# Matmuls on zeros before the first tile, w2 loaded behind the first seven x tiles, and the h3T tile placed first in its pool, in a one-core attention and MLP kernel

## The chip, the cores and the metric

The kernel runs on one core of a Trainium2 chip. The metric is the device time of one execution in microseconds (us). One execution moves by a few us from run to run (six runs of the unchanged kernel: 1540.59 to 1544.17 us). Each kernel also has one profiled execution. Its trace gives the start and length of every instruction, what ended each wait, and each DMA packet. Engines are named as in the profile: PE is TensorE (matmuls), PEld its weight loads, DVE VectorE, ACT ScalarE, POOL GpSimd, and SP the engine that issues most DMAs (SPq is its queue).

## The reference, cut to what matters

The result is the sum of x, a memory-augmented attention A and a block B, both fed by the layer norm of x. The change touches only B, which runs first:

```python
def _B_ref(x, w1, w2, w3, w4):                 # x is the layer norm of the input, 2048 x 1024
    h = _gelu(_layernorm(x) @ w1)              # stage 1
    # four quarters of h shifted by +1, -1, +2, -2 tokens
    hs = shifted(h) @ w2                       # stage 2
    x1 = x + hs
    return x1 + _gelu(_layernorm(x1) @ w3) @ w4   # stage 3 (w3, w4)
```

## The kernel before: the parts that matter

The 2048 tokens are 16 tiles of 128. In stage 1 every tile is normalized twice over (`xn2` for w1, `xn` kept for later), `xn2` is transposed, and PE multiplies by w1. Tiles 0 to 7 are transposed by PE, tiles 8 to 15 by DMA transposes issued from SP. Groups of tiles go through PE in order: tile 0, tile 1, then pairs (2,3), (4,5), and so on. PE must have tiles 8 and 9 transposed to start the sixth group. The trace calls the kept tile `xnk`; PE first reads it in a small matmul with `c_segsum` (sums over segments of tokens). `hTB` is what stage 1 writes, and the tiles `ps`, in PSUM, are what the matmuls write.

```python
load_x(0)
for c in range(2):
    nc.sync.dma_start(w1_sb[:, :, c * 512:(c + 1) * 512], w1_v[:, :, c * 512:(c + 1) * 512])
    load_x(c + 1)
for n in range(3, 7):
    load_x(n)
...
def norm1(n):                                   # xn of tile n; frees the buffer of x tile n
    ...
    nc.vector.tensor_scalar(xn, xts[n][:], mv[:, 0:1], rr[:, 0:1], op0=ALU.subtract, op1=ALU.mult)
    nc.gpsimd.dma_start(xn_v[:, n, :], xn)
    load_x(n + 7)
    if n < 4:
        nc.sync.dma_start(w2_sb[:, 2 * n:2 * n + 2, :], w2_v[:, 2 * n:2 * n + 2, :])
    elif n in (12, 15):
        load_w3()
...
norm_stats(0)                                   # DVE: statistics of x tile 0
xn2 = norm2(0, t0, 0)
norm_stats(1, 0)                                # DVE: first half of the statistics of tile 1
transposes(xn2, t0, 0, 0)                       # PE
transposes(xn2, t0, 0, 1, on_dve=True)          # PE, copied out by DVE
norm_stats(1, 1)
...
# stage 2, per tile: matmuls on w2, norm, then
    nc.scalar.activation(xn3[:], x1[:], ACTF.Identity, bias=nm3[:], scale=r3[:])
    nc.sync.dma_start_transpose(xn3T[n // 4][:, n % 4], xn3[:])
# stage 3 takes over the memory of stages 1 and 2
big = p3.enter_context(tc.tile_pool(name="p3big", bufs=1))
w4_sb = big.tile([P, FT, D], BF16)
...
h3T = big.tile([P, FT, 512], BF16)
...
    nc.scalar.activation(h3T[:, f, :], ps[:], ACTF.Gelu_apprx_tanh)   # after eight matmuls on w3
```

A tile pool is a stack region of on-chip memory. When a new pool lies where a closed one lay, the framework makes the first users of its tiles wait for the last users of the old memory.

## Time and profile before

| what | value |
|---|---|
| time, six runs | 1540.59 to 1544.17 us, median 1542.38 |
| span of the profiled execution | 1545.1 us |
| PE busy | 1514.8 us (98%) |
| first matmul on w1, w3, w4 | 8.23, 131.97, 181.93 us |

The first line of the page's part 1 reads: busy us, share of the span, instructions.

```profile
PE 1514.8 (98%) x10308; PEld 839.7 (54%) x10382; DVE 523.8 (34%) x1092; ACT 513.9 (33%) x1218; POOL 192.5 (12%) x272
```

PE is the limit, so only time in which PE waits, or runs slowly, can be won. The waits view of PE over the whole span (who waited for what: us in total, times, longest; some lines left out):

```profile
PE ps L283 <- DVE xn L262: 6.9, 1, 6.9
PE psO L678 <- DMA PT<-Pn: 3.8, 5, 1.6
PE ps L569 <- ACT Vs L571: 3.1, 1, 3.1
PE ps L300 <- DMA xn2T<-xn: 1.5, 1, 1.5
PE ps L515 <- ACT h3T L516: 1.1, 1, 1.1
PE ps L292 <- DVE xnk L271: 0.8, 1, 0.8
```

The three edits aim at three things seen here: the 6.9 us before PE's first instruction and the slow clock that follows it, the DMA traffic of the start, and the 1.1 us wait for h3T. The timeline shows each (start us, us, engine, line, operation, in brackets the idle time before it and its releaser). The start:

```profile
8.03 0.69 DVE L247 BATCH_NORM_STATS2 st<-xt 128x6 f32<-128x512 bf16 x1 [1.14 <-DMA xt<-in_A_x_dram]
9.37 3.15 PE L300 MATMUL ps<-xn2T,w_sb 128*128 128x128 bf16 x28 [0.55 <-DVE xn2T L285]
17.96 0.54 DVE L271 TENSOR_SCALAR xnk<-xt,mv,rr 128x1024 bf16<-128x1024 bf16 x1
18.55 0.35 PE L292 MATMUL ps<-c_segsum_sb,xnk 128*128 128x4 bf16 x8 [0.81 <-DVE xnk L271]
```

28 matmuls took 3.15 us, 112 ns each. Sixteen of the same shape at 18.77 us started 56 ns apart. The Trainium skill (TensorE: Matmul & The Clock Gate, "Part 1: The HAM clock gate") says that the array starts at half rate until it has been busy for a window of about 3.4 us. The trace's clock record agrees: full rate from 13.99 us on, after a window (10.58 to 13.99 us) in which PE was busy throughout. Yet at 18.55 us PE stands and waits for VectorE, whose chain began when x tile 1 landed at 8.03 us.

The one wait for a DMA transpose, and the h3T wait:

```profile
46.77 1.47 PE L300 MATMUL ps<-xn2T,w_sb 128*128 128x256 bf16 x12 [1.50 <-DMA xn2T<-xn]
139.45 2.06 ACT L516 ACTIVATE h3T<-ps 128x512 bf16<-128x512 f32 x4 [3.01 <-DMA xn3T<-xn]
140.10 1.24 PE L515 MATMUL ps<-xn3T,w_sb 128*128 128x512 bf16 x5 [1.06 <-ACT h3T L516]
```

The first line is PE's start on tiles 8 and 9. The other two say that ACT may not write h3T before the last xn3 transpose has landed, and that PE runs out of PSUM buffers meanwhile.

The windows view gives the DMA load. Columns: stretch, its length, busy us (and count) of PE, PEld, DVE, ACT, POOL, granted clock, mean busy share of the 16 DMA engines, GB/s.

```profile
12.00:14.00 2.00, 2.00 (x21) 2.00 (x20) 1.90 (x6) 1.30 (x3) 0.08 (x1) 1.00 0.54 205
14.00:16.00 2.00, 2.00 (x39) 2.00 (x37) 1.90 (x6) 1.17 (x6) 0.82 (x2) 1.00 0.00 0
28.00:30.00 2.00, 2.00 (x23) 1.82 (x21) 1.90 (x6) 1.24 (x3) 0.66 (x1) 1.00 1.07 383
```

DMA is idle around 15 us and full at 28 us, where the w2 loads run. (The clock column reads 1.00 before the first record of a change and says nothing there.)

### The profile page before, as it was taken

How to read it: one execution, taken by the hardware profiler on the slowest of the kernel's cores; microseconds unless marked ns; L12 is line 12 of the kernel's file. 1: busy time of each engine (PE TensorE's matmuls, PEld its weight loads, DVE VectorE, ACT ScalarE, POOL GpSimd, SP SyncE). 2: the span in 40 equal slices, each digit the busy share in tenths (PEclk: the TensorE clock that was granted, in tenths of full speed). 3: DMA queues.
4: the chain of work that ended last, by engine and by line, in shares of the span. 5: the costliest groups of instructions: out<-in, count | busy, mean ns of one | idle time of the engine just before them, and what ended most of it. 6: DMA issues, size and time to landing. Idle time of an engine off the chain costs nothing. (4 is left out here: it accounts for less than half of the span.)

```text
span 1545.1 us, 25390 instructions
## 1 busy us (share of the span) xinstructions
PE 1514.8 (98%) x10308; PEld 839.7 (54%) x10382; DVE 523.8 (34%) x1092; ACT 513.9 (33%) x1218; POOL 192.5 (12%) x272
## 2 busy tenths in 40 slices
PE   7999999999999999999999999999999999999998
PEld 7844444444444444444456645654665566466654
DVE  8284010000200111111246624651663365235541
ACT  5533202103012011111156614651662366056620
POOL 5232020221211241010000011002000200100001
PEclk9999999999999999999999999999999999999999
DMA  7679543452353998542389947992997599458611
GB/s 251 182 213 311 205 148 125 143 184 83 130 164 87 215 275 273 173 124 83 123 231 252 235 129 179 246 237 73 239 239 175 129 249 227 111 130 198 136 45 50
DMA packets 288601, 270.39 MB, mean 175 GB/s; under 512 B 137459, under 2 KB 255368, under 8 KB 288480
## 3 DMA queue, kind: packets, MB, share of 16 engines
q1 hardware_dynamic: 265088, 185.53, 47.0%
q0 software_dynamic: 23392, 83.19, 16.8%
q8 instruction: 83, 1.36, 0.4%
q14 instruction: 38, 0.31, 0.1%
HBM read 190.73 MB, written 46.73 MB: 154 GB/s over the span
## 5 line engine op out<-in xcount | busy, mean ns | idle before, releaser
L639 PE MATMUL ps<-hTb,wt 128*128 128x396 bf16 (+2 forms) x3072 | 514.9, 314 | 1.3 <-DMA wt<-in_A_Wq_dram 1.3
L639 PEld LDWEIGHTS <-wt 128*128 128x128 bf16 x3072 | 264.5, 97 | 148.1 <-DMA wt<-in_A_Wq_dram 2.1
L569 PE MATMUL ps<-wt,xT 128*128 128x512 bf16 x1004 | 222.0, 381 | 4.1 <-ACT Vs L571 3.1
L697 PE MATMUL pso<-wo_sb,oX 128*128 128x512 bf16 x1000 | 223.2, 379 | 1.4 <-issue 0.2
L515 PE MATMUL ps<-xn3T,w_sb 128*128 128x512 bf16 x896 | 195.9, 379 | 1.1 <-ACT h3T L516 1.1
L540 PE MATMUL ps<-w_sb,h3T 128*128 128x512 bf16 x872 | 194.3, 379 | 1.2
L569 PEld LDWEIGHTS <-xT 128*128 128x128 bf16 x1024 | 100.6, 98 | 125.3 <-issue 5.6
L516 ACT ACTIVATE h3T<-ps 128x512 bf16<-128x512 f32 x112 | 66.5, 597 | 292.0 <-PE ps L515 289.0
L697 PEld LDWEIGHTS <-oX 128*128 128x128 bf16 x1024 | 98.9, 98 | 115.3
L645 ACT CAST KT<-ps 128x396 bf16<-128x396 f32 (+1 forms) x192 | 87.1, 456 | 189.6 <-PE ps L639 186.5
L515 PEld LDWEIGHTS <-w_sb 128*128 128x128 bf16 x896 | 86.8, 98 | 103.9 <-issue 1.3
L540 PEld LDWEIGHTS <-h3T 128*128 128x128 bf16 x896 | 86.8, 98 | 102.8
L660 DVE TENSOR_REDUCE sums<-sm 99x4 f32<-99x396 f32 (+1 forms) x176 | 97.6, 555 | 113.9 <-ACT sm L658 113.9
L647 ACT ACTIVATE QT<-ps 128x396 bf16<-128x396 f32 (+1 forms) x192 | 89.4, 469 | 108.0 <-PE ps L639 79.8
L656 DVE TENSOR_TENSOR sm<-psS,c_mask_reg_sb 99x396 f32<-99x396 f32 x160 | 91.4, 572 | 90.1 <-PE psS L654 89.9
L571 ACT CAST Vs<-ps 128x512 bf16<-128x512 f32 x64 | 37.2, 586 | 238.4 <-PE ps L569 152.6
L658 ACT ACTIVATE sm<-sm 99x396 f32<-99x396 f32 (+1 forms) x176 | 92.7, 527 | 65.9 <-DVE sm L656 64.7
L573 DVE CAST Vs<-ps 128x512 bf16<-128x512 f32 x64 | 44.2, 692 | 181.8 <-PE ps L569 156.8
L666 DVE TENSOR_TENSOR Pn<-sm,rs 99x396 bf16<-99x396 f32 (+1 forms) x176 | 99.0, 562 | 10.2 <-DMA PT<-Pn 4.0
L541 DVE TENSOR_TENSOR R<-ps,R 128x512 f32<-128x512 f32 x32 | 22.1, 692 | 231.4 <-PE ps L540 215.0
L704 POOL DMA_DIRECT2D out_dram<-ot x32 | 17.5, 546 | 575.8 <-DVE ot L703 569.9
L679 ACT CAST oX<-psO 128x384 bf16<-128x384 f32 x176 | 82.5, 469 | 16.8 <-PE psO L678 16.7
(116 smaller groups left out, 979.5 us busy)
## 6 DMA issues: line engine op xcount, KB each, us to landing
wt<-in_A_Wq_dram SPq DMA_DIRECT2D x78, 512.0 KB
wt<-in_A_Wk_dram SPq DMA_DIRECT2D x78, 512.0 KB
wt<-in_A_Wv_dram POOLq DMA_DIRECT2D x24, 1024.0 KB, 7.1
V_scratch<-Vs SPq DMA_DIRECT2D x32, 512.0 KB
V<-V_scratch SPq DMA_DIRECT2D x40, 384.0 KB
w_sb<-in_B_w_dram SPq DMA_DIRECT2D x9, 1024.0 KB
R_scratch<-x POOLq DMA_DIRECT2D x16, 512.0 KB, 4.4
R<-R_scratch SPq DMA_DIRECT2D x16, 512.0 KB
```

The costliest lines, as they stand in the source:

```text
L515: nc.tensor.matmul(ps[:].rearrange("p (n t) -> p n t", t=P), w3_sb[:, k, f * P:(f + 1) * P], xn3T[tb][:, :, k, :], start=(k == 0), stop=(k ...
L540: nc.tensor.matmul(ps[:], h3T[:, f, j * P:(j + 1) * P], w4_sb[:, f, ch * 512:(ch + 1) * 512], start=(f == 0), stop=(f == FT - 1))
L569: nc.tensor.matmul(ps[:], xT[:, m4 * 4 + j, k, :], wv[:, k, :], start=(k == 0), stop=(k == KT - 1))
L639: nc.tensor.matmul(ps[:, :nb] if B["b"] in (0, 5) else ps[:, :nb].rearrange("p (t c) -> p t c", t=4), w[:, k, hh * P:(hh + 1) * P], B["rhs ...
L645: nc.scalar.copy(o, i)
L647: nc.scalar.mul(o, i, scale)
L656: nc.vector.tensor_tensor(sm[:T, :, :T], S3, t["mask"][:].unsqueeze(1).to_broadcast((T, 4, T)), op=ALU.add)
L658: nc.scalar.activation(e[:T, :, :T], sm[:T, :, :T], ACTF.Exp, scale=LN2)
L660: nc.vector.tensor_reduce(ss, e[:T, :, :T], axis=AX.X, op=ALU.add)
L666: nc.vector.tensor_tensor(Pn[:T, :, :T], e[:T, :, :T], rs[:T, :].unsqueeze(2).to_broadcast((T, 4, T)), op=ALU.mult)
L679: nc.scalar.copy(oX[:, hs_, t["tok"]:t["tok"] + nt], O3[:, :, 0:nt])
L697: nc.tensor.matmul(self.ps[:], self.oX[:, h, self.gl * P:(self.gl + 1) * P], wo_sb[:, h, self.cc], start=(h == 0), stop=(h == H - 1))
```

## The change

The intent: PE's clock is to be warm when the first tile arrives; w2 (2 MB) is to fill the DMA hole before 20 us rather than the crowded stretch after it; and h3T, first in its pool, comes to lie on memory that only PE used, so that its first write needs no transpose to finish.

```diff
                     for n in range(3, 7):
                         load_x(n)
+                    for i in range(4):
+                        nc.sync.dma_start(w2_sb[:, 2 * i:2 * i + 2, :], w2_v[:, 2 * i:2 * i + 2, :])
 ...
                         load_x(n + 7)
-                        if n < 4:
-                            nc.sync.dma_start(w2_sb[:, 2 * n:2 * n + 2, :], w2_v[:, 2 * n:2 * n + 2, :])
-                        elif n in (12, 15):
+                        if n in (12, 15):
                             load_w3()
 ...
+                    wz = big.tile([P, 512], BF16)
+                    nc.vector.memset(wz[:], 0.0)
+                    for _ in range(3):
+                        ps = psum.tile([P, 512], F32, tag="mm", bufs=4, name="warm")
+                        for i in range(4):
+                            nc.tensor.matmul(ps[:], wz[:, :P], wz[:], start=(i == 0), stop=(i == 3))
                     norm_stats(0)
 ...
                 big = p3.enter_context(tc.tile_pool(name="p3big", bufs=1))
+                h3T = big.tile([P, FT, 512], BF16)
                 w4_sb = big.tile([P, FT, D], BF16)
 ...
-                h3T = big.tile([P, FT, 512], BF16)
```

## The prediction

> **What bounds the kernel now.** TensorE: the page's first part gives PE 1514.8 us busy of a 1545.1 us span (98%). The waits view leaves PE little to win: 6.9 us before its first instruction, then 3.8 us (five waits for transposed probabilities), 3.1 us (value stage), 1.5 us (DMA-transposed xn2T), 1.3, 1.1 us (first h3T write), 0.8 us, and pieces. The three edits touch only the first 140 us.
>
> **Part 1, twelve matmuls on zeros.** They end by about 6.5 us (memset near 1 us, then twelve 128x512 matmuls at an estimated 0.43 us each: four times the 0.11 us that the 128x128 ones take below), just before the first transposes at 6.95 us, so they add nothing. They are to warm the clock. The Trainium skill (TensorE: Matmul & The Clock Gate, "Part 1: The HAM clock gate") says the array runs at half rate until about 3.4 us of sustained work. The trace agrees: in the timeline 28 matmuls of 128 columns took 3.15 us (112 ns each) at 9.4 to 12.5 us; at 18.8 us the same shape ran at 56 ns; the clock record rises at about 14 us. About 3 us of cold time can go. But that stretch hangs on VectorE: its statistics for tile 1 start at 8.03 us, when x1 lands behind half of w1, and from there VectorE is busy almost without a gap to 40 us. PE stands 0.8 us at 18.55 us until VectorE writes the first xnk tile (ended 18.50). No VectorE instruction after 8 us waits for PE. So PE arrives earlier and waits longer: the 0.8 us wait grows to 1 to 2 us, waits of about 1 us appear before the transposes of tiles 1 and 2, and 18.55 us stays. Worth about 0 (0 to 0.3).
>
> **Part 2, w2 early.** The windows view shows DMA busy 0.54 at 12-14 us and 0.00 to 0.25 at 14-20 us, then 0.84 to 1.35 from 20 to 46 us, where 2 MB of w2 compete with x, the xn writes and the DMA transposes. The transpose of tile 9 is issued at 38.1 us and releases PE only at 46.77 us, after 1.5 us of PE idle. With w2 (four 512 KB loads; estimated 6 us at the trace's 350 GB/s) moved into the hole, transposes 8 and 9 land several us earlier and this wait goes. From 18.55 to 45.3 us PE is otherwise its own limit, and after 46.8 us it runs without a gap to 124 us. Worth 1.5 us, all on the critical path.
>
> **Part 3, h3T first.** Intent: h3T's first write waits for an earlier stage's xn3 transpose (ScalarE 3.0 us, PE 1.06 us at 139.0-140.1 us). Moved, h3T's address lies inside the old hTB, which only PE reads. But in the built programs the first h3T write carries the same DMA waits with the same counts in both kernels: the wait is set per pool, not per address. Worth 0; the 1.06 us stays.
>
> **Sum.** Before averaged 1542.5 us; minus 1.5 gives 1541.0 us, range 1538.0 to 1544.0. One re-throttled clock window (3.4 us at half rate near 598 us, after a 3 us wait in the value stage) may come or go and move a run by about 1.7 us. Chances: faster by over 2% 0.005, same 0.99, slower 0.005.
>
> **What would show it.** Stage 1's first 128-column matmuls near 56 ns; PE's wait for xnk over 0.8 us, still ending near 18.5 us; no PE wait for xn2T; the w2 matmuls starting near 75.4 instead of 76.9 us; ScalarE's first h3T write still released by the xn3 transpose, PE idle about 1 us.
>
> **What would make it wrong.** VectorE speeding up; the DMA transposes staying slow for their own reasons; new contention delaying x1 to x6; a shift near 598 us.

## The result, and the profile after

The changed kernel took 1540.05 us (median of six runs, 1538.61 to 1542.54), the kernel before 1542.38 us (median of six). The ratio is 0.9982 with a 95% interval of 0.9968 to 0.9997. Kernels are compared only within the same rounds. Ratios here are not quite the ratio of the medians quoted. That is the same within 2%, inside the predicted range, and 0.5 to 4.9 us faster.

The waits view of PE over the whole span, after (some lines left out, among them 1.3 us before the zeros, for their memset):

```profile
PE ps L575 <- ACT Vs L577: 3.0, 1, 3.0
PE ps L283 <- DVE xn L264: 1.6, 2, 0.9
PE ps L521 <- ACT h3T L522: 1.1, 1, 1.1
PE ps L300 <- DVE xn2T L285: 1.0, 1, 1.0
PE ps L292 <- DVE xnk L273: 0.8, 1, 0.8
PE psO L684 <- DMA PT<-Pn: 0.8, 2, 0.6
```

The wait for the transpose (xn2T, DMA) is gone. The waits for xnk and for h3T stand as before. The timeline of the changed kernel, the lines that answer to those of before:

```profile
7.93 0.69 DVE L249 BATCH_NORM_STATS2 st<-xt 128x6 f32<-128x512 bf16 x1 [1.14 <-DMA xt<-in_A_x_dram]
9.27 3.04 PE L300 MATMUL ps<-xn2T,w_sb 128*128 128x128 bf16 x28 [0.97 <-DVE xn2T L285]
18.45 0.35 PE L292 MATMUL ps<-c_segsum_sb,xnk 128*128 128x4 bf16 x8 [0.81 <-DVE xnk L273]
137.77 1.57 ACT L522 ACTIVATE h3T<-ps 128x512 bf16<-128x512 f32 x3 [3.02 <-DMA xn3T<-xn]
138.42 0.81 PE L521 MATMUL ps<-xn3T,w_sb 128*128 128x512 bf16 x3 [1.07 <-ACT h3T L522]
```

The 28 matmuls ran at 109 ns each (3.04 us over 28), still slow. The clock record says why: full rate at 5.23 us, half rate again from 8.65 to 12.06 us, full from then on. The windows view shows the two clock windows and the new DMA load:

```profile
5.23:8.65 3.42, 1.75 (x16) 0.87 (x15) 1.44 (x4) 1.35 (x2) 0.82 (x2) 1.00 1.00 346
8.65:12.06 3.41, 2.79 (x27) 2.79 (x27) 2.49 (x7) 1.35 (x4) 0.80 (x3) 0.50 1.06 393
14.00:16.00 2.00, 1.44 (x26) 1.26 (x23) 1.90 (x7) 1.11 (x4) 0.81 (x2) 1.00 1.04 405
28.00:30.00 2.00, 2.00 (x23) 1.81 (x21) 1.90 (x7) 1.24 (x3) 0.77 (x1) 1.00 0.68 241
```

So w2 did move into the hole (DMA 0.00 to 1.04 at 14 to 16 us, 1.07 to 0.68 at 28 to 30 us). Where the difference of the two profiled executions (1545.1 and 1538.6 us) lies is told by the starts of the stages in the timelines:

| from | to | before, us | after, us | difference |
|---|---|---|---|---|
| span's start | first matmul on xnk | 18.55 | 18.45 | -0.10 |
| first matmul on xnk | first on w3 | 113.42 | 111.83 | -1.59 |
| first on w3 | first on w4 | 49.96 | 49.97 | 0.01 |
| first on w4 | first of the attention's value stage | 363.70 | 363.71 | 0.01 |
| value stage | first query projection | 225.95 | 225.81 | -0.14 |
| first query projection | PE's last matmul | 767.53 | 762.82 | -4.71 |

The second row is the predicted 1.5 us. The last row was not predicted and no edit touches that stage. Both had to be tested.

### The profile page after: what moved, and what is told of

The parts are those of the page before. It is cut to its first block, busy times and chain, and to the rows that moved or that the text cites. A ratio compares the mean times of both kernels' runs of the same rounds, so it can differ in the third digit from the quotient of the medians.

```text
span 1538.6 us, 25489 instructions
## 1 busy us (share of the span) xinstructions
PE 1521.2 (99%) x10394; PEld 839.8 (55%) x10394; DVE 524.1 (34%) x1093; ACT 513.4 (33%) x1218; POOL 192.5 (13%) x272
```

## The experiments

Three measures were used. Whole times need many runs. The interval "first xnk matmul to first w3 matmul" from a profile is 111.75 to 112.02 us whenever PE does not wait for a transpose in it, so it shows tenths of a us. And the packet records of the trace show when the 1024 packets of each DMA transpose start. The four kernels that were run without rounds have a single run each; intervals of their profiles are used, their whole times are not.

### Each part alone: e1_warm, e2_w2_early, e3_h3T_first

Each is the kernel before plus one part of the diff above: the zeros (`wz` and the loop over `warm`), the w2 lines, or the two h3T lines.

> The kernel before plus the twelve matmuls on zeros alone. My theory (the start hangs on VectorE, which waits for x1): the first transposes may take about 0.6 instead of 1.04 us, but PE's segment-sum matmul on the first xnk tile still starts at 18.4 to 18.6 us and the first matmul on w2 at 76.7 to 77.0 us as before (76.93); whole time within noise of before (0 to -0.3 us). Rival (the slow clock costs about 3 us at the start): the first w2 matmul comes 2 to 3 us earlier, near 74 to 75 us.

> The kernel before with the w2 loads behind the first seven x tiles, no zeros, no move of h3T. My theory: this is the whole gain. The PE wait of 1.5 us for the DMA transpose of tile 9 is gone and the first stage 3 matmul (on w3) starts at 130.1 to 130.5 us instead of 131.97; whole time 1.5 to 1.9 us less than before. Rival (the three parts share the gain): 0.5 us or less here.

> The kernel before with h3T placed first in its pool and nothing else. My theory (the wait is the pool's, not the tile's): ScalarE's first h3T write is still released by the DMA transpose of the last xn3 tile after about 3.0 us of idle, and PE still stands about 1.06 us there; whole time within noise of before. Rival (the address decides): PE's wait is gone, 1.06 us saved.

Measured whole times, against seven runs of before: 0.9983 (0.9955 to 1.0012), 0.9986 (0.9958 to 1.0014), 0.9984 (0.9955 to 1.0013). All three look alike, the h3T move too, which changes only addresses. These times cannot tell the parts apart.

**Zeros alone.** Here the clock record stood at full rate from 6.61 us with no fall. The timeline:

```profile
9.24 1.72 PE L300 MATMUL ps<-xn2T,w_sb 128*128 128x128 bf16 x28 [0.72 <-DVE xn2T L285]
11.89 0.62 PE L283 MATMUL ps<-c_ident_sb,xn 128*128 128x128 bf16 x8 [0.92 <-DVE xn L262]
16.09 0.40 PE L283 MATMUL ps<-c_ident_sb,xn 128*128 128x128 bf16 x4 [0.90 <-DVE xn L262]
18.42 0.35 PE L292 MATMUL ps<-c_segsum_sb,xnk 128*128 128x4 bf16 x8 [0.82 <-DVE xnk L271]
```

The 28 matmuls now took 1.72 instead of 3.15 us, and PE spent what it won waiting for VectorE, 0.92 us before tile 1 and 0.90 us before tile 2. It reached xnk at 18.42 us, against 18.55. Up to xnk the warm clock is worth nothing, shown with the clock fully warm. Where the last 0.13 us came from, these runs do not tell; runs of one and the same kernel lie further apart than that in their stages.

What did surprise: the wait for the transpose of tile 9 was also absent in this kernel and in e3_h3T_first (111.75 and 112.02 us from xnk to w3), though both load w2 late, exactly as before does. The first w2 matmul of e1_warm thus came at 74.92 us instead of 76.93: my expectation (76.7 to 77.0) was missed, and the rival's number (74 to 75) came out, though not by the rival's way, since xnk came when it had before and 1.50 of the 2.01 us are the missing wait. My reason for the 1.5 us was in doubt from here on.

**h3T alone.** The timeline shows the old wait, unchanged:

```profile
138.51 2.06 ACT L516 ACTIVATE h3T<-ps 128x512 bf16<-128x512 f32 x4 [3.00 <-DMA xn3T<-xn]
139.16 1.67 PE L515 MATMUL ps<-xn3T,w_sb 128*128 128x512 bf16 x7 [1.06 <-ACT h3T L516]
```

**w2 alone** had 111.92 us from xnk to w3, no transpose wait, as expected. It also met a bad draw of the h3T wait:

```profile
141.19 2.13 PE L515 MATMUL ps<-xn3T,w_sb 128*128 128x512 bf16 x6 [3.60 <-ACT h3T L516]
```

PE stood 3.60 us, the clock fell to half rate for one window (141.82 to 145.23 us by its record), and the w3-to-w4 interval was 54.18 us instead of 49.97. The h3T wait was 1.1 us in the other profiles with the shared pool, so it can grow.

### A pool of its own for h3T: e4_h3T_own_pool and e4_again

The changed kernel with one more edit. The address of h3T is the same.

```diff
+                h3T = p3.enter_context(tc.tile_pool(name="p3h", bufs=1)).tile([P, FT, 512], BF16, name="h3T")
                 big = p3.enter_context(tc.tile_pool(name="p3big", bufs=1))
-                h3T = big.tile([P, FT, 512], BF16)
                 w4_sb = big.tile([P, FT, D], BF16)
```

The built programs show what ACT's first h3T write waits for (semaphore counts of DMAs; HW are those issued by SP, among them the last four xn3 transposes, SW those of POOL, the writes of stage 2 among them):

```
before:   SW0..5 >= 80, SW6,7 >= 64, HW0,1 >= 112, HW6,7 >= 96, DVE >= 203, PE >= 1032
changed:  SW0..5 >= 80, SW6,7 >= 64, HW0,1 >= 112, HW6,7 >= 96, DVE >= 204, PE >= 1044
own pool: SW2..5 >= 48, DVE >= 201, PE >= 1044
```

Before and changed differ only by the added memset and the twelve matmuls.

> The changed kernel with h3T in a pool of its own at the same address as in the changed kernel; the built program's wait list of the first h3T write then holds no transposes of xn3. My theory: PE's wait of 1.07 us at 137.4 to 138.4 us is gone, ScalarE's first h3T write follows its own normalization of the last tile (near 134.8 us), and the w4 stage starts at 179.0 to 179.3 us instead of 180.24; whole time about 1.1 us under the changed kernel, about 2.7 under before. Rival (the transposes of xn3 or something else hold PE anyway): the w4 stage starts near 180.2 us.

The timeline of the second profile of this kernel (e4_again):

```profile
129.95 6.42 PE L521 MATMUL ps<-xn3T,w_sb 128*128 128x512 bf16 x29
131.88 0.60 ACT L522 ACTIVATE h3T<-ps 128x512 bf16<-128x512 f32 x1 [0.90 <-DVE mv L389]
133.19 1.24 ACT L397 ACTIVATE xn<-x,nm,r 128x1024 bf16<-128x1024 f32 x1 [0.71 <-POOL nm L395]
```

ACT writes the first h3T at 131.9 us, ahead of its own last normalization (I had expected it behind), and PE runs through. The w3-to-w4 interval is 48.74 us in both profiles, and in a third kernel with this edit, against 49.97: 1.23 us won, the same to 0.01 us each time. So the wait belonged to the pool, not to the address, and the first placement in the shared pool could not remove it. In whole time the first call gave 0.9978 (0.9949 to 1.0007), so more rounds were run:

> The changed kernel with h3T in its own pool once more, as the version that should beat both: no PE wait for the transpose of tile 9, none at the first h3T write, 103.8 to 104.2 us from the first w2 matmul to the first w4 matmul instead of 105.0 to 105.2. Whole time 1 to 2.5 us under before (ratio 0.9984 to 0.9994) if the later stages' chance waits average out; the interval will be about 0.002 either way, so it may not be told from 1.

e4_again: median 1540.66 us against 1544.96 us (eleven runs of before), ratio 0.9974, interval 0.9953 to 0.9994. It beats the kernel before clear of noise. Of these 4 us the h3T edit accounts for 1.23 by the profiles; most of the rest is not explained. It was not timed in the same rounds as the changed kernel; that it beats that one rests on the 1.23 us of the profiles. No PE wait was left in the stretch from 120 to 180 us.

### The controls: before_again, after_again

Both kernels once more, unchanged.

> The kernel before once more, unchanged: a null control. The single-part runs have shown the 1.5 us PE wait for the transpose of tile 9 absent in two kernels that load w2 late as before does (zeros alone, h3T alone), so my prediction's mechanism is in doubt. New theory (the wait is a near miss that comes and goes: the last packet of that transpose starts at 43.4 to 45.5 us and PE wants it at about 45.0 us): the wait is between 0 and 1.5 us, more likely 0, and the first w2 matmul follows PE's first segment-sum matmul by 56.5 to 56.8 us when there is no wait (58.38 us in the first profile of before). Old theory (late w2 causes the wait): the wait is there again, 1.2 to 1.8 us. Whole time over the runs of before of the same rounds: ratio 0.998 to 1.002; how far from 1 it falls shows what whole times can tell apart.

> The changed kernel once more, to see whether its gain repeats. No wait for the transpose of tile 9 under either theory, 56.5 to 56.8 us between PE's first segment-sum matmul and the first w2 matmul, h3T wait of PE about 1.1 us. Whole time: new theory 0 to 1 us under before (ratio 0.9993 to 1.0002 apart from noise), old theory 1.5 us or more under it (0.9990 or less).

before_again took a median of 1544.19 us and after_again 1543.68 us, with 1543.6 us for eleven runs of before. The ratios: 1.0 (0.998 to 1.002) and 0.9999 (0.998 to 1.0017). Five rounds therefore resolve about 3 us, and the gain of the first measurement did not repeat in whole time. The profile of after_again met its expectation (no transpose wait), and its clock did not fall back: the 28 matmuls took 1.72 us (61 ns each), and xnk still came at 18.22 us after a wait of 0.82 us. In the profile before_again had the transpose wait again:

```profile
46.25 0.92 PE L300 MATMUL ps<-xn2T,w_sb 128*128 128x256 bf16 x7 [1.12 <-DMA xn2T<-xn]
```

### When does the transpose of tile 9 come late? before_third, before_fourth, e5_w3_too, e6_w2_late

Two more profiles of before, one kernel with nearly twice the bytes in the crowded stretch, and one with w2 moved away from it, to later:

```diff
 # e5_w3_too: two w3 loads move from tiles 12 and 15 to tiles 1 and 2
-                        elif n in (12, 15):
+                        if n in (1, 2):
                             load_w3()
 # e6_w2_late: w2 behind the transposes of tiles 10 to 13
-                        if n < 4:
-                            nc.sync.dma_start(w2_sb[:, 2 * n:2 * n + 2, :], w2_v[:, 2 * n:2 * n + 2, :])
-                        elif n in (12, 15):
+                        if 10 <= n < 14:
+                            i = n - 10
+                            nc.sync.dma_start(w2_sb[:, 2 * i:2 * i + 2, :], w2_v[:, 2 * i:2 * i + 2, :])
+                        if n in (12, 15):
                             load_w3()
```

> The kernel before, another profile. So far the PE wait for the transpose of tile 9 stood in 3 of 5 profiles with w2 loaded late (1.50 and 1.12 us in the kernel before, 1.93 us with two w3 loads added; none with zeros alone or h3T alone) and in 0 of 5 with w2 loaded early. If late w2 makes the near miss more likely: a wait of 0 to 1.6 us, and the last packet of that transpose later than the 43.4 to 44.5 us of the early-w2 profiles. If it always stands: 1.1 to 1.6 us.

> The kernel before, one more profile, in a call of its own with the best version. PE wait for the transpose of tile 9 between 0 and 1.6 us, as in the other profiles of before; 56.5 to 56.8 us from PE's first segment-sum matmul to the first w2 matmul if there is no wait, 57.6 to 58.4 us if there is.

> The kernel before with two of the w3 loads (1.8 MB together) moved forward among the w2 loads, at tiles 1 and 2, so nearly twice the bytes fall into the stretch from 19 to 34 us. New theory (in the kernel before the w2 bytes had just been moved when the first transpose came, its packets start as its issue ends at 35.5 us, so w2 cost nothing; more bytes do not fit): transposes 8 and 9 land 3 to 5 us later and PE waits 2 to 5 us for xn2T or the x tiles; first w2 matmul near 78 to 80 us. Rival (these transposes are paced by their own issue and packets, not by bandwidth): the first w2 matmul stays at 75 to 77 us.

> The kernel before with the four w2 loads moved later, behind the transposes of tiles 10 to 13, so that neither w2 nor anything in its place crosses the stretch before the transpose of tile 9. If what counts is keeping w2 out of the stretch from 19 to 34 us: no wait for the transpose of tile 9, its last packet at 43.4 to 44.5 us as with early w2, the first w2 matmul 56.5 to 56.8 us after PE's first segment-sum matmul, unless w2 now delays the transposes of tiles 11 to 13 (their slack is 3 us or more). If early arrival itself were what counts: the wait stays.

All profiles but that of e7, which comes below. "Packets" are the starts of the first and the last packet of the transpose of tile 9; "wait" is PE's wait for it.

| kernel | w2 | zeros | packets, us | wait, us | xnk to w3, us |
|---|---|---|---|---|---|
| before | late | no | 42.31 to 45.48 | 1.50 | 113.42 |
| before_again | late | no | 41.20 to 45.44 | 1.12 | 113.04 |
| before_third | late | no | 42.47 to 44.10 | 0 | 111.75 |
| before_fourth | late | no | 41.84 to 43.93 | 0.61 | 112.53 |
| e1_warm | late | yes | 41.96 to 43.45 | 0 | 111.75 |
| e3_h3T_first | late | no | 42.93 to 44.86 | 0 | 112.02 |
| changed | early | yes | 42.02 to 43.67 | 0 | 111.83 |
| after_again | early | yes | 41.67 to 43.48 | 0 | 111.83 |
| e2_w2_early | early | no | 42.38 to 44.49 | 0 | 111.92 |
| e4_h3T_own_pool | early | yes | 41.91 to 43.38 | 0 | 111.76 |
| e4_again | early | yes | 41.72 to 43.28 | 0 | 111.76 |
| e5_w3_too | late, and w3 | no | 45.76 to 46.71 | 1.93 | 115.45 |
| e6_w2_late | behind tile 10 | no | 41.04 to 44.78 | 1.05 | 114.06 |

Three things follow. First, the wait is a near miss, not a fixed cost: of the six profiles with w2 where before has it, three have it, with early w2 none of five (nor the sixth, below). The packet times alone do not decide: in the five profiles with the wait PE started 0.8 to 1.8 us after the last packet's start, and before_fourth waited although its last packet came earlier than that of e3_h3T_first, because PE was ahead there (xnk at 18.04 us, in e3_h3T_first at 19.01). The six late ones average 112.42 us, the five early ones 111.82: early w2 goes with 0.6 us less, not with 1.5.

Second, no w2 bytes stand in front of tile 9 in the kernel before. Its first packets start at nearly the same time, 42.0 us in the changed kernel and 42.3 us in the kernel before. The transpose of tile 8, issued at 34.0 and 34.1 us, starts its packets at 35.5 us in both, the moment its issue ends, so nothing was queued in front of it by then. Tile 9's packets do start late, 0.7 to 2.7 us after its issue ends, but in every kernel: three x loads are issued between the two transposes. What differs is how long its packets take from first to last start, 1.5 to 4.2 us in the profiles with late w2 and 1.5 to 2.1 us with early w2. And in e6_w2_late the wait is there with no w2 byte moved before it:

```profile
45.93 3.67 PE L301 MATMUL ps<-xn2T,w_sb 128*128 128x256 bf16 x32 [1.05 <-DMA xn2T<-xn]
```

The data packets of its first w2 load start at 46.7 us, as tile 10's transpose ends. That agrees with the Trainium skill (DMA: Bandwidth & Descriptors, "Queues, rings and completion order"): each DMA engine takes the descriptors of a ring in order, and this load stood behind that transpose. What traffic was around tile 9 were the x loads of tiles 13 to 15 and the xn writes, which every kernel has. The interval of e6_w2_late, 114.06 us, also holds a second wait, 0.93 us at 61.81 us: the transpose of tile 13, issued behind the third moved w2 load, had its last packet at 61.06 us (58.43 us in the kernel before).

Third, bandwidth does matter once more is asked of that stretch. With 1.8 MB of w3 added, tile 8's packets ran to 43.1 us (38.2 us in the kernel before), PE waited, and the first w2 matmul came at 78.71 us, as expected:

```profile
48.53 3.67 PE L300 MATMUL ps<-xn2T,w_sb 128*128 128x256 bf16 x32 [1.93 <-DMA xn2T<-xn]
```

So the stretch had room for w2 but not for 1.8 MB more; this is one profile.

What stays open is why early w2 met no late transpose. With these counts (3 of 6 against 0 of 5) luck is not ruled out: the four kernels of the first experiments, two with late and two with early w2, had no such wait at all. The zeros are a rival at least as strong. None of the six profiles with zeros has the wait, and only e1_warm (zeros, late w2) and e2_w2_early (early w2, no zeros) hold the two edits apart, one profile each, neither with a wait. The packets lean to the zeros: from first to last start the transpose of tile 9 took 1.47 to 1.81 us in all six profiles with zeros and 1.63 to 4.24 us in the seven without (e5_w3_too left out), e2_w2_early with 2.11 us among these. One fetch of instructions splits the same way in the packet records: 8 KB on queue 14 took 1.8 to 2.3 us, starting at 36.3 to 37.3 us, in the seven, and 0.3 us, starting at 37.8 to 40.1 us, in the six. Whether it holds up the transpose no run shows. More profiles of e1_warm and e2_w2_early would be the next test.

### x1 ahead of w1: e7_x1_first_own_pool

If VectorE's chain from x1 sets the start, x1 should land first. The edit, on top of the own pool:

```diff
                     load_x(0)
+                    load_x(1)
                     for c in range(2):
                         nc.sync.dma_start(w1_sb[:, :, c * 512:(c + 1) * 512], w1_v[:, :, c * 512:(c + 1) * 512])
-                        load_x(c + 1)
+                    load_x(2)
```

> The changed kernel with h3T in its own pool, and x1 loaded ahead of both halves of w1 instead of between them. My theory (VectorE's chain from x1 sets the start): statistics of tile 1 begin at about 6.8 us instead of 7.93, PE's first segment-sum matmul at 17.2 to 17.5 us instead of 18.45, first w2 matmul at 73.7 to 74.1 us instead of 75.0; with the h3T wait gone the w4 stage starts at 177.6 to 178.1 us instead of 180.24. Rival (w1 then comes too late and PE waits for it, or the later pace is not set by that chain): first w2 matmul at 74.7 us or later. Whole time about 2 us under the changed kernel if the first holds.

```profile
6.68 0.69 DVE L250 BATCH_NORM_STATS2 st<-xt 128x6 f32<-128x512 bf16 x1
10.34 3.59 PE L301 MATMUL ps<-xn2T,w_sb 128*128 128x128 bf16 x32 [2.89 <-DMA w_sb<-in_B_w_dram]
13.75 0.69 DVE L250 BATCH_NORM_STATS2 st<-xt 128x6 f32<-128x512 bf16 x1 [2.93 <-DMA xt<-in_A_x_dram]
```

The rival won. Tile 1's statistics began at 6.68 us as hoped, but PE's first matmul on w1 came 2.4 us later than in the changed kernel (10.34 against 7.92 us) and x2 later still, and PE reached xnk at 20.43 us instead of 18.45. VectorE's chain set the start here too, now from x2: its statistics of tile 2 began 1.98 us later than in the changed kernel (13.75 against 11.77 us), and so did PE's work on xnk. The order alone does not account for so much: up to the first half of w1 1.5 MB were to land, as many as up to x1 in the changed kernel, where they were there at 7.93 us. The packet records show the reads slow from 3.5 to 8.5 us, 62 to 160 KB per half us against 125 to 189 KB in the changed kernel. One profile cannot say whether the order caused that. From xnk to w3 it took 111.75 us with early w2, no wait. Whole time: 0.9992 (0.997 to 1.0013).

### The late stage

The 4.71 us between the first query projection and the last matmul are not explained. Four profiles of the unchanged kernel gave 767.53, 765.63, 766.80 and 769.00 us there, a spread of 3.4 us. The six kernels with early w2 gave 762.82, 763.95, 765.75, 768.36, 764.02 and 763.13 us, 764.7 on average, and the eight others 767.0. That is 2.3 us apart, and four of the six lie under all of the eight. PE's waits for transposed probabilities make up most of it: 0.8, 1.6, 3.1, 3.9, 1.7 and 1.0 us in the six, 3.6 to 5.1 us in the eight. Luck is an unlikely account of that split, though it was looked for after the fact. But the repeated whole times (0.9999) do not show it, I know of no path from the first 140 us to it, and it stays open.

## Why the prediction was right or wrong, point by point

**The number** was right: 1541.0 us predicted, 1540.05 us measured, range 1538.0 to 1544.0. By the profiles part of that agreement is luck, as follows.

**Part 1, zeros: right in worth up to xnk, wrong in two signs.** "Worth about 0" holds for the path that the prediction describes: xnk came at 18.42 us in e1_warm, with the clock fully warm from 6.61 us. Whether the zeros act on the transpose of tile 9 is open. But "Stage 1's first 128-column matmuls near 56 ns" failed in the changed kernel's profile (109 ns), because the clock fell back at 8.65 us; it held roughly in e1_warm and after_again (61 ns). And "the 0.8 us wait grows to 1 to 2 us" failed: it stayed 0.81 us, since the matmuls between tile 2's transposes and xnk were never cold. The slack shows upstream, before tiles 1 and 2, as the same sentence also said.

**Part 2, w2: the step that failed.** The prediction said that w2's bytes "compete with x, the xn writes and the DMA transposes", that without them "transposes 8 and 9 land several us earlier", and put this at 1.5 us, "all on the critical path". w2 did move as said. But tile 8's transpose met no queue in either kernel, and tile 9's first packet came 0.3 us earlier, its last 1.8 us earlier. The wait came in three of four profiles of before, with 1.50, 1.12 and 0.61 us, so the 1.5 us was one draw read as a fixed cost. The term measured 0.6 us on average (112.42 against 111.82 us), of which some or all may be luck or the zeros' doing, and the cause given is not needed for the wait: e6_w2_late has it without w2 ahead of it. What makes tile 9's packets slow stays open. I read a busy DMA share of about 1 as a backlog of w2. Where the packets of tile 8's transpose start the moment its issue ends, none is left.

**Part 3, h3T: right.** "The wait is set per pool, not per address", worth 0, the 1.06 us stays: 1.07 us after, 1.06 us in e3_h3T_first, and gone with a pool of its own.

**The sum.** The means of the six runs each differ by 2.3 us (1542.47 and 1540.17), more than the 1.5 predicted, but the repeat gave nothing (0.9999). In the first stages the profiles with early w2 lie some 0.6 us under the others, which may be luck; the rest of the first measurement lies in the late stage and is not explained.

## What to carry to other kernels

A wait that one profile shows once may be a draw. Take two or three profiles of the unchanged kernel before building on its size, and compare intervals between fixed instructions where whole times are too noisy. Warming or speeding an engine is worth nothing while another's chain, here VectorE from the landing of x1, sets its next start: look for the wait downstream of the slow stretch. And where a new tile inherits a wait from the pool it lies in, read the built program's wait list before and after: a move within the pool left it as it was, and a separate pool removed it.

## What the Trainium skill lacked or had wrong

- TensorE: Matmul & The Clock Gate, Part 1, names an idle window of about 3.4 us for the fall to half rate. Here a window in which PE was busy for 1.75 of 3.42 us (5.23 to 8.65 us of the changed kernel) was followed by one at half rate. No share of busy time is given there. With windows of 3.41 us laid from each profile's first clock record, in the 14 profiles no window at full rate with 1.78 us or more of busy PE was followed by half rate and every one with 1.29 us or less was; in between both occurred (1.52 us in e5_w3_too stayed, the 1.75 us above fell). Every window at half rate with 2.76 us or more was followed by full rate, none with 2.61 us or less. The window length agrees: 3.41 us in every record of half rate between two full ones, but one of two windows' length in e7_x1_first_own_pool.
- The same part does not say whether matmuls on zeros warm the clock. They do: they started at 1.26 us in the changed kernel, and the record rose at 5.23 us.
- DMA: Bandwidth & Descriptors, "Latency and other measured facts", gives 261 GB/s for a DMA transpose with a non-contiguous middle dimension and about 350 to 400 GB/s for a contiguous one, and nothing on how that varies beside other traffic. The packets of one 256 KB transpose took 0.95 us (e5_w3_too) to 4.2 us (before_again) from first to last start, an estimate of 276 down to 62 GB/s from those times.
